# Converting double-precision weights by integer steps in a fused attention and SwiGLU kernel

## Chip, core and metric

The kernel runs on one core of a Trainium2 chip. The core has a matrix engine (TensorE, PE in the profile), a vector engine (VectorE, DVE), an activation engine (ScalarE, ACT), a general engine (GpSimd, POOL) and a queue that issues its transfers (SyncE, SP). The metric is the device time of one execution in microseconds (us). A difference under 0.5% can't be told from no change here.

## What is computed

The reference, cut to what matters:

```
a    = softmax(phi, over the 576 positions)            # phi (8, 8, 576, 32)
k_m, v_m = a^T k, a^T v                                # 32 memory rows per head
attn = softmax(q k_m^T / 8);  x = attn v_m             # 4608 rows x 512
xn   = x / sqrt(mean(x*x) + 1e-6) * rms_g
g, val = xn @ w_gate, xn @ w_val                       # w_*: (512, 1536)
out  = (g * sigmoid(g) * val) @ w_out                  # w_out: (1536, 512)
```

The inputs q, k, v, phi are float32, and the weights reach the core as 8-byte doubles: a low and a high 32-bit word for each number. The core has to make float32 of them itself.

## The kernel before

**Two stages.** The first stage, about 0 to 145 us, reads phi, k, v and q, builds the memory rows of all 8 batches and, for the first 4 batches, the attention weights. The second stage has 48 steps `i`: two passes over the 12 column blocks of the weights, each pass for two pairs of batches (`where(i)` gives pass, block pair `u`, batch pair `pr` and block `j`). A step multiplies a weight block by the value rows (`vw_steps`, 12 matmuls at L849), splits that product into a high and a low part (`xh` on ScalarE at L873, `xl` on VectorE at L874), multiplies it by the attention weights to get gate and value (`gv_steps`, 48 matmuls at L896), applies SiLU (`sg`, L904) and the product (`hf`, L905), splits again (`hh` L918, `hl` L919), and every second step multiplies by w_out (`out_steps`, 54 matmuls at L938, summed into `acc` at L943 on ScalarE or L945 on VectorE). The attention of the last 4 batches (L965 to L1035) is woven into the first pass.

**Conversion.** `convert(kind, n)` makes float32 of one 128x512 weight tile, kind 0 for w_gate, 1 for w_val, 2 for w_out; 12 blocks make 36 tiles. It happens in the first pass only; split tiles are stored to memory and loaded again in the second pass (`reload`). Before, a tile takes steps `s0` to `s4`. From the high word: the exponent bits by a mask (L345), clamped (L347), rescaled on ScalarE (L350), joined with the sign bit (L358). From both words: the fraction by a mask (L365), the low word added to it (L369), scaled to a number between 1 and 2 on ScalarE (L376). A product of the two (L385) is the weight `w`. That is six VectorE instructions, of which two tiles' last one runs on GpSimd (`PRM["CE"]`), and two on ScalarE. `s5` splits `w` into high (ScalarE, L402) and low (GpSimd, L403), `s6` stores them. `raw` tiles come from memory into two buffers; `ex` and `mi` have one buffer each, so that a tile's steps can start only when the tile before has let go of it.

**Order.** All pieces are placed on a time axis by the table `PRM` (offsets in `PRE`, `PSW`, `PI` for the conversions) and recorded in that order; the framework's scheduler then fixes the order on each engine. Each engine runs its list strictly in order.

**The first step.** For `i == 0` the value product has two one-bank PSUM tiles with the tag `o`; all other steps have one two-bank tile with the tag `vw`, of which there is one buffer. The banks of `vw` belong in the first stage to the tag `tr`, whose last user is the normalisation of the second batch pair (`rp`, read by VectorE at L212).

Of the kernel before, what the change touches and what calls it, by code (L numbers as in the profile page):

```python
# [1 line left out]

# [88 lines left out]
def kernel(  # L91
# [243 lines left out]
    def convert(kind, n):  # L335
# [4 lines left out]

        def s0():
            d["raw"] = t = raw.pop((kind, n))
            hw = t[:, :, 1]
# [1 line left out]
            V.tensor_scalar(out=ex, in0=hw, scalar1=0x7FF00000, scalar2=None, op0=ALU.bitwise_and)  # L345
            if (kind < 2 and n < 2 and PRM["CA"]) or ((kind == 2 or n >= 2) and PRM["CB"]):
                V.tensor_scalar(  # L347
                    out=ex, in0=ex, scalar1=float(896 << 20), scalar2=float(1151 << 20), op0=ALU.max, op1=ALU.min
                )
                nc.scalar.activation(ex, ex, AF.Copy, scale=8.0, bias=-float(896 << 23))  # L350
            else:
                V.tensor_scalar(out=ex, in0=ex, scalar1=float(-896 << 20), scalar2=0.0, op0=ALU.add, op1=ALU.max)

        def s1():
# [3 lines left out]
            V.scalar_tensor_tensor(  # L358
                out=ex, in0=d["raw"][:, :, 1], scalar=-(1 << 31), in1=ex,
                op0=ALU.bitwise_and, op1=ALU.bitwise_or,  # L360
            )

        def s2():
            d["m"] = m = wp[0].tile([P, 512], I32, tag="mi", name=f"mi{nm}")
            V.tensor_scalar(  # L365
                out=m, in0=d["raw"][:, :, 1], scalar1=0xFFFFF, scalar2=None, op0=ALU.bitwise_and
            )
# [1 line left out]
            V.scalar_tensor_tensor(  # L369
                out=mf, in0=d["raw"].bitcast(U32)[:, :, 0], scalar=2.0 ** -32, in1=m,  # L370
                op0=ALU.mult, op1=ALU.add,
            )
# [8 lines left out]

        def s4():
            m, ex = d["m"].bitcast(F32), d["ex"].bitcast(F32)
            on_pool = n < 2 and kind < 2 and PRM["CE"][n] & (1 << kind)
            (nc.gpsimd if on_pool else V).tensor_tensor(out=d["w"], in0=m, in1=ex, op=ALU.mult)  # L385
# [444 lines left out]
    def vw_steps(i):  # L830
# [2 lines left out]

        def mm(cc):
            def f():

# [8 lines left out]
                for e in range(2):
                    def lhs(vt):
                        return vt[:, cc, e].rearrange("p o x -> p (o x)")
                    for n, (l, r) in enumerate(((vh, wh), (vh, wl), (vl, wh))):
                        nc.tensor.matmul(  # L849
                            vp[:, e, :], lhs(l), r[:, 2 * cc + e, :],  # L850
                            start=(n == 0), stop=(n == 2),
                        )
            return f

        def evac():
            xh = sb.tile([P, 2, 2, 256], F32R, tag="xh", name=f"xh{i}", bufs=2)
            xl = sb.tile([P, 2, 2, 256], F32R, tag="xl", name=f"xl{i}", bufs=2)
            if i == 0:
                for cc, vp in enumerate(vw[i]):
                    halves = ((slice(0, 64), vp[:64]), (slice(64, P), vp[64:, ::-1, :]))  # L860
                    for rows, src in halves:
                        nc.scalar.copy(xh[rows, cc], src)
                    for rows, src in halves:
                        nc.vector.tensor_tensor(
                            out=xl[rows, cc], in0=src, in1=xh[rows, cc].bitcast(F32), op=ALU.subtract
                        )
                vw[i] = xh, xl
# [258 lines left out]
```

## Time and profile before

| what | value |
|---|---|
| time, median of 3 runs | 913.88 us (913.27 to 917.01) |
| span of the profiled execution, first to last instruction | 912.9 us |
| what lies around the span, by the median | about 1.0 us |
| TensorE busy | 837.6 us, 92% of the span |
| VectorE busy | 600.1 us, 66%, 1028 instructions |
| ScalarE busy | 421.2 us, 46% |
| GpSimd busy | 284.6 us, 31% |
| moved by transfers | 106.41 MB, mean 117 GB/s |

A row of a group gives the count, the busy time, the mean duration of one, and then the idle time of the engine just before these instructions with what ended it. A row of the table by windows gives, for each stretch, the busy time and count on each engine, the granted TensorE clock as a share of full speed, and the transfers. Matmuls overlap, so that a busy TensorE need not be one at its peak rate.

### The profile page before, as it was taken

The numbers are of one execution on the slowest core, as the hardware profiler recorded it, in microseconds if no ns is written. First come the engines' busy times: TensorE is split into PE (matmuls) and PEld (weight loads), VectorE is DVE, ScalarE is ACT, GpSimd is POOL, SyncE is SP. The second block draws the span as 40 slices with busy tenths as digits, with TensorE's granted clock in tenths as the row PEclk, the third lists the DMA queues.
The fourth block names the chain that finished last, engine by engine and source line by source line (L and its number), as shares of the span: only waits on it lengthen the run. The fifth ranks groups of instructions, "written<-read, shape, count | busy, mean of one in ns | idle before, by whom it ended". The sixth has DMA issues, their size and how long they took to land.

```text
span 912.9 us, 15844 instructions
## 1 busy us (share of the span) xinstructions
PE 837.6 (92%) x6207; PEld 740.8 (81%) x6207; DVE 600.1 (66%) x1028; ACT 421.2 (46%) x719; POOL 284.6 (31%) x242
## 2 busy tenths in 40 slices
PE   4989586899997999989999999999999999999997
PEld 4777475788886798878888897798889999999996
DVE  5578959998897876978765564732445454454543
ACT  2657334777755454666443352354424233243330
POOL 3464735432413233324232151312112121121120
PEclk9899788999999999999999999999999999999999
DMA  8976554354454341543314034311304013040046
GB/s 277 329 260 227 199 165 142 105 172 118 163 153 129 108 119 60 145 129 125 115 58 139 12 105 139 91 60 47 93 1 139 1 47 93 1 139 1 1 114 140
DMA packets 81506, 106.41 MB, mean 117 GB/s; under 512 B 34324, under 2 KB 52248, under 8 KB 81432
## 3 DMA queue, kind: packets, MB, share of 16 engines
q1 hardware_dynamic: 81432, 105.41, 37.6%
q8 instruction: 49, 0.80, 0.4%
q14 instruction: 25, 0.20, 0.1%
HBM read 73.93 MB, written 31.46 MB: 115 GB/s over the span
## 4 chain that ended last, share of the span: by engine, by line
PE 64%; DVE 20%; issue 5%; ACT 5%; DMA 4%; POOL 1%; SPq 0%; DVEq 0%; ACTq 0%; POOLq 0%
PE po L938 26%; PE pv L896 12%; PE pg L896 12%; PE vp L849 6%; PE kvp L573 3%; DVE xl L874 2%; DVE ex L345 2%; DVE mi L365 2%; DVE mi L369 2%; DVE ex L358 2%; DMA phi<-in_phi_dram 2%; DVE w L385 1%; PE xp L235 1%; DVE ex L347 1%; DVE acc L945 1%
## 5 line engine op out<-in xcount | busy, mean ns | idle before, releaser
L919 POOL TENSOR_TENSOR hl<-hf,hh 128x512 fp32r<-128x512 f32 (+1 forms) x96 | 139.8, 1457 | 422.3 <-ACT hh L918 409.3
L945 DVE TENSOR_TENSOR acc<-po,acc 128x512 f32<-128x512 f32 x180 | 123.0, 686 | 131.2 <-PE po L938 130.6
L938 PE MATMUL po<-oh,hh 128*128 128x512 f32 x432 | 174.0, 404 | 8.1 <-DVE acc L945 3.8
L938 PE MATMUL po<-ol,hh 128*128 128x512 f32 x432 | 170.8, 395 | 0.0
L938 PE MATMUL po<-oh,hl 128*128 128x512 f32 x432 | 170.7, 395 | 0.0
L904 ACT ACTIVATE sg<-pg 128x256 f32<-128x256 f32 x192 | 78.4, 409 | 161.7 <-PE pg L896 139.9
L874 DVE TENSOR_TENSOR xl<-vp,xh 64x1024 fp32r<-64x1024 f32 x94 | 114.7, 1220 | 47.9 <-ACT xh L873 46.4
L905 DVE TENSOR_TENSOR hf<-pv,sg 128x256 f32<-128x256 f32 x192 | 85.5, 453 | 72.4 <-PE pv L896 51.6
L873 ACT CAST xh<-vp 64x1024 fp32r<-64x1024 f32 x94 | 94.6, 1006 | 47.0 <-PE vp L849 22.4
L918 ACT CAST hh<-hf 128x512 fp32r<-128x512 f32 (+1 forms) x96 | 64.5, 673 | 85.2 <-DVE hf L905 59.4
L938 PEld LDWEIGHTS po<-oh,hh 128*128 128x128 f32 x432 | 81.3, 189 | 24.7 <-DVE acc L945 6.1
L938 PEld LDWEIGHTS po<-oh,hl 128*128 128x128 f32 x432 | 81.4, 189 | 19.6
L896 PE MATMUL pg<-ath,xh 128*128 128x320 f32 (+1 forms) x384 | 87.0, 300 | 9.3 <-ACT sg L904 4.9
L849 PE MATMUL vp<-wh,vm 128*128 128x256 f32 x384 | 85.6, 287 | 5.8 <-DVE xl L874 4.7
L938 PEld LDWEIGHTS po<-ol,hh 128*128 128x128 f32 x432 | 81.6, 189 | 11.0
L896 PE MATMUL pv<-ath,xh 128*128 128x320 f32 (+1 forms) x384 | 85.0, 300 | 2.6 <-DVE hf L905 2.4
L896 PE MATMUL pg<-ath,xl 128*128 128x320 f32 (+1 forms) x384 | 85.0, 296 | 0.1
L896 PE MATMUL pg<-atl,xh 128*128 128x320 f32 (+1 forms) x384 | 85.0, 296 | 0.0
L896 PE MATMUL pv<-atl,xh 128*128 128x320 f32 (+1 forms) x384 | 84.5, 296 | 0.0
L896 PE MATMUL pv<-ath,xl 128*128 128x320 f32 (+1 forms) x384 | 83.9, 296 | 0.0
L896 PEld LDWEIGHTS pg<-ath,xh 128*128 128x128 f32 x384 | 63.7, 189 | 16.4 <-ACT sg L904 7.1
L849 PEld LDWEIGHTS vp<-wh,vm 128*128 128x128 f32 x384 | 65.8, 190 | 9.7 <-DVE xl L874 2.7
(131 smaller groups left out, 1382.2 us busy)
## 6 DMA issues: line engine op xcount, KB each, us to landing
kv<-in_k_dram SPq DMA_DIRECT2D x32, 288.0 KB, 4.9
kv<-in_v_dram SPq DMA_DIRECT2D x32, 288.0 KB, 5.3
out_dram<-acc SPq DMA_DIRECT2D x72, 128.0 KB, 2.4
raw<-in_moe_w_gate_dram SPq DMA_DIRECT2D x12, 512.0 KB, 3.8
raw<-in_moe_w_val_dram SPq DMA_DIRECT2D x12, 512.0 KB, 3.7
wd<-wh SPq DMA_DIRECT2D x12, 512.0 KB, 3.0
wd<-wl SPq DMA_DIRECT2D x12, 512.0 KB, 3.3
raw<-in_moe_w_out_dram SPq DMA_DIRECT2D x12, 512.0 KB, 3.7
```

The lines of the kernel that those rows point to most:

```text
L345: V.tensor_scalar(out=ex, in0=hw, scalar1=0x7FF00000, scalar2=None, op0=ALU.bitwise_and)
L573: nc.tensor.matmul(kvp[64 * par:64 * par + 64, cc, 0:128], e_bd[j][:, hp, c, :], st["kv", b, hp][:, :, 64 * c:64 * c + 64], start=(c == 0) ...
L849: nc.tensor.matmul(vp[:, e, :], lhs(l), r[:, 2 * cc + e, :], start=(n == 0), stop=(n == 2),)
L873: nc.scalar.copy(xh[rows], src)
L874: nc.vector.tensor_tensor(out=xl[rows], in0=src, in1=xh[rows].bitcast(F32), op=ALU.subtract)
L896: nc.tensor.matmul(pt[:, :N], l[:, cc, b, half * P:half * P + P], r[:, b, cc, t0:t0 + n, :].rearrange("p t x -> p (t x)"), start=(m == 0), ...
L904: nc.scalar.activation(sg[:, :N], pg[:, :N], AF.Silu)
L905: nc.vector.tensor_tensor(out=hf[:, :, b, :], in0=pv[:, :N].rearrange("p (t x) -> p t x", x=64), in1=sg[:, :N].rearrange("p (t x) -> p t x ...
L918: nc.scalar.copy(hh, hv)
L919: nc.gpsimd.tensor_tensor(out=hl, in0=hv, in1=hh.bitcast(F32), op=ALU.subtract)
L938: nc.tensor.matmul(po, l[:, tt, :], r, start=(m == 0), stop=(m == 5))
L945: nc.vector.tensor_tensor(out=accs[key], in0=po, in1=accs[key], op=ALU.add)
```

## The change

`convert` is rewritten. The high word is read as a float32 on ScalarE (`Abs`), clamped on VectorE between two float constants whose bits are the old integer bounds, shifted left by 3 and masked, and joined with the two top bits of the raw word. The low word's top three bits, rounded, come from a ScalarE copy with a scale of 2^-29 into an integer tile. An integer addition of the two is the weight's bit pattern. That is four VectorE instructions a tile (or three and one on GpSimd) in place of six, and two on ScalarE as before; both ScalarE instructions now stand at the head of a tile and read `raw` from it. In the built program the addition on VectorE is an instruction on 16-bit halves, 1024 of them a partition. In the first step the value product is the two-bank tile that all others have.

```diff
+EXP_LO = struct.unpack("f", struct.pack("I", 896 << 20))[0]
+EXP_HI = struct.unpack("f", struct.pack("I", (1151 << 20) - 1))[0]
...
         def s0():
             d["raw"] = t = raw.pop((kind, n))
-            hw = t[:, :, 1]
             d["ex"] = ex = wp[0].tile([P, 512], I32, tag="ex", name=f"ex{nm}")
-            V.tensor_scalar(out=ex, in0=hw, scalar1=0x7FF00000, scalar2=None, op0=ALU.bitwise_and)
...
-                V.tensor_scalar(
-                    out=ex, in0=ex, scalar1=float(896 << 20), scalar2=float(1151 << 20), op0=ALU.max, op1=ALU.min
-                )
-                nc.scalar.activation(ex, ex, AF.Copy, scale=8.0, bias=-float(896 << 23))
...
+            nc.scalar.activation(ex.bitcast(F32), t.bitcast(F32)[:, :, 1], AF.Abs)
+            V.tensor_scalar(
+                out=ex.bitcast(F32), in0=ex.bitcast(F32), scalar1=EXP_LO, scalar2=EXP_HI,
+                op0=ALU.max, op1=ALU.min,
+            )
+            d["m"] = m = wp[0].tile([P, 512], I32, tag="mi", name=f"mi{nm}")
+            nc.scalar.activation(m, t.bitcast(U32)[:, :, 0], AF.Copy, scale=2.0 ** -29)

         def s1():
...
+            V.tensor_scalar(
+                out=ex, in0=ex, scalar1=3, scalar2=0x3FFFFFFF,
+                op0=ALU.logical_shift_left, op1=ALU.bitwise_and,
+            )
+        def s2():
             V.scalar_tensor_tensor(
-                out=ex, in0=d["raw"][:, :, 1], scalar=-(1 << 31), in1=ex,
+                out=ex, in0=d["raw"][:, :, 1], scalar=-(1 << 30), in1=ex,
                 op0=ALU.bitwise_and, op1=ALU.bitwise_or,
             )
-            V.tensor_scalar(
-                out=m, in0=d["raw"][:, :, 1], scalar1=0xFFFFF, scalar2=None, op0=ALU.bitwise_and
-            )
-            V.scalar_tensor_tensor(
-                out=mf, in0=d["raw"].bitcast(U32)[:, :, 0], scalar=2.0 ** -32, in1=m,
-                op0=ALU.mult, op1=ALU.add,
-            )

         def s3():
-            nc.scalar.activation(mf, mf, AF.Copy, scale=2.0 ** -20, bias=1.0)
...
         def s4():
-            (nc.gpsimd if on_pool else V).tensor_tensor(out=d["w"], in0=m, in1=ex, op=ALU.mult)
+            (nc.gpsimd if on_pool else V).tensor_tensor(out=d["w"].bitcast(I32), in0=d["m"], in1=d["ex"], op=ALU.add)
...
-                if i == 0:
-                    vw.setdefault(i, []).append(o_tile(f"vp{i}_{cc}").rearrange("p (e f) -> p e f", e=2))
-                elif cc == 0:
+                if cc == 0:
                     whole = ps.tile([P, 2, 2, 256], F32, tag="vw", name=f"vp{i}", bufs=1)
...
-            if i == 0:
-                for cc, vp in enumerate(vw[i]):
-                    ...  # four copies (L862), four subtractions (L864) of 64x512
-                return
```

The new instructions move the order. In the rows that follow, `ex2_0` is the tile `ex` of kind 2, block 0, and likewise `mi`, `w` and `raw_20`; `vp0` is the value product of step 0, `xh0` and `xl0` its parts.

VectorE where the first stage hands over to the second, before:

```order
L212 TENSOR_TENSOR at1_1503<-at1_1503,rp1_4_1770 128x1024
L385 TENSOR_TENSOR w1_1_1735<-mi1_1_1731,ex1_1_1726 128x512
L212 TENSOR_TENSOR at1_1503<-at1_1503,rp1_8_1776 128x256
L345 TENSOR_SCALAR ex2_0_1836<-raw_20_1724 128x512
L365 TENSOR_SCALAR mi2_0_1841<-raw_20_1724 128x512
L347 TENSOR_SCALAR ex2_0_1836<-ex2_0_1836 128x512
L369 SCALAR_TENSOR_TENSOR mi2_0_1841<-raw_20_1724,mi2_0_1841 128x512
L864 TENSOR_TENSOR xl0_1827<-vp0_0_1812,xh0_1826 64x512 x2
L358 SCALAR_TENSOR_TENSOR ex2_0_1836<-raw_20_1724,ex2_0_1836 128x512
L864 TENSOR_TENSOR xl0_1827<-vp0_1_1819,xh0_1826 64x512 x2
L385 TENSOR_TENSOR w2_0_1847<-mi2_0_1841,ex2_0_1836 128x512
```

and after:

```order
L217 TENSOR_TENSOR at1_1502<-at1_1502,rp1_4_1762 128x1024
L379 ISA w1_1_1727<-mi1_1_1723,ex1_1_1720 128x1024
L217 TENSOR_TENSOR at1_1502<-at1_1502,rp1_8_1768 128x256
L350 TENSOR_SCALAR ex2_0_1823<-ex2_0_1823 128x512
L359 TENSOR_SCALAR ex2_0_1823<-ex2_0_1823 128x512
L366 SCALAR_TENSOR_TENSOR ex2_0_1823<-raw_20_1718,ex2_0_1823 128x512
L379 ISA w2_0_1832<-mi2_0_1826,ex2_0_1823 128x1024
L854 TENSOR_TENSOR xl0_1818<-vp0_1804,xh0_1817 64x1024
L350 TENSOR_SCALAR ex2_1_1962<-ex2_1_1962 128x512
L359 TENSOR_SCALAR ex2_1_1962<-ex2_1_1962 128x512
L366 SCALAR_TENSOR_TENSOR ex2_1_1962<-raw_21_1733,ex2_1_1962 128x512
L854 TENSOR_TENSOR xl0_1818<-vp0_1804,xh0_1817 64x1024
```

The whole of tile 2_0 now stands ahead of the first `xl0`, and three steps of tile 2_1 between the two halves of `xl0`.

ScalarE at the same place, before:

```order
L402 CAST wh1_1720<-w1_1_1735 128x4x128
L223 CAST ath1_1783<-at1_1503 128x2x64 x2
L862 CAST xh0_1826<-vp0_0_1812 64x512 x2
L350 ACTIVATE ex2_0_1836<-ex2_0_1836 128x512
L862 CAST xh0_1826<-vp0_1_1819 64x512 x2
L376 ACTIVATE mi2_0_1841<-mi2_0_1841 128x512
L402 CAST oh0_2035<-w2_0_1847 128x512
L873 CAST xh1_1901<-vp1_1849 64x1024
L904 ACT_TABLE_LOAD
L904 ACTIVATE sg0_00_1871<-pg0_00_1857 128x256
```

and after:

```order
L396 CAST wh1_1714<-w1_1_1727 128x4x128
L349 ACTIVATE ex2_0_1823<-raw_20_1718 128x512
L355 ACTIVATE mi2_0_1826<-raw_20_1718 128x512
L228 CAST ath1_1775<-at1_1502 128x2x64 x2
L853 CAST xh0_1817<-vp0_1804 64x1024
L349 ACTIVATE ex2_1_1962<-raw_21_1733 128x512
L355 ACTIVATE mi2_1_1965<-raw_21_1733 128x512
L396 CAST oh0_2018<-w2_0_1832 128x512
L853 CAST xh0_1817<-vp0_1804 64x1024
L349 ACTIVATE ex0_2_2048<-raw_02_1830 128x512
L355 ACTIVATE mi0_2_2051<-raw_02_1830 128x512
L884 ACT_TABLE_LOAD
```

Between the two halves of `xh0` stand two conversion steps of tile 2_1 and the copy `oh0` of tile 2_0's weight, and the head of tile 0_2 stands ahead of the first SiLU.

VectorE in the middle of the first pass, block 7 of w_gate, before:

```order
L385 TENSOR_TENSOR w1_6_3673<-mi1_6_3667,ex1_6_3656 128x512
L345 TENSOR_SCALAR ex0_7_3750<-raw_07_3598 128x512
L365 TENSOR_SCALAR mi0_7_3756<-raw_07_3598 128x512
L347 TENSOR_SCALAR ex0_7_3750<-ex0_7_3750 128x512
L874 TENSOR_TENSOR xl10_3473<-vp10_3399,xh10_3472 64x1024
L369 SCALAR_TENSOR_TENSOR mi0_7_3756<-raw_07_3598,mi0_7_3756 128x512
L945 TENSOR_TENSOR acc0_5_2329<-po5_5_3106,acc0_5_2329 128x512
L358 SCALAR_TENSOR_TENSOR ex0_7_3750<-raw_07_3598,ex0_7_3750 128x512
L1012 TENSOR_REDUCE mx2_3_0_3168<-S2_3_0_3157 128x10
L874 TENSOR_TENSOR xl10_3473<-vp10_3399,xh10_3472 64x1024
L385 TENSOR_TENSOR w0_7_3762<-mi0_7_3756,ex0_7_3750 128x512
```

and after:

```order
L379 ISA w1_6_3628<-mi1_6_3616,ex1_6_3613 128x1024
L992 TENSOR_REDUCE mx2_3_5_3168<-S2_3_5_3134 128x8
L854 TENSOR_TENSOR xl10_3435<-vp10_3360,xh10_3434 64x1024
L993 TENSOR_TENSOR ex2_3_3119<-S2_3_5_3134,mx2_3_5_3168 128x256
L350 TENSOR_SCALAR ex0_7_3705<-ex0_7_3705 128x512
L925 TENSOR_TENSOR acc0_6_2399<-po5_6_3171,acc0_6_2399 128x512
L359 TENSOR_SCALAR ex0_7_3705<-ex0_7_3705 128x512
L1005 TENSOR_REDUCE sm2_3_3225<-ex2_3_3119 128x18
L366 SCALAR_TENSOR_TENSOR ex0_7_3705<-raw_07_3556,ex0_7_3705 128x512
L1006 TENSOR_SCALAR sm2_3_3225<-sm2_3_3225 128x18
L925 TENSOR_TENSOR acc0_7_2414<-po5_7_3185,acc0_7_2414 128x512
L379 ISA w0_7_3715<-mi0_7_3708,ex0_7_3705 128x1024
```

The four steps of a tile keep their place among the work that TensorE waits for (`acc`, `xl`); the two masks at its head and the fraction's sum are gone.

More of the change, by code (lines that the diff above doesn't have):

```diff
@@ L1 @@
+import struct
 from contextlib import ExitStack, nullcontext
@@ L354, in s1 @@
+            V.tensor_scalar(
[4 more added lines that the diff above has]
+            nc.scalar.activation(m, t.bitcast(U32)[:, :, 0], AF.Copy, scale=2.0 ** -29)
         def s1():
             ex = d["ex"]
-            if not ((kind < 2 and n < 2 and PRM["CA"]) or ((kind == 2 or n >= 2) and PRM["CB"])):
-                V.tensor_scalar(out=ex, in0=ex, scalar1=float(255 << 20), scalar2=8.0, op0=ALU.min, op1=ALU.mult)
+            V.tensor_scalar(
+                out=ex, in0=ex, scalar1=3, scalar2=0x3FFFFFFF,
+                op0=ALU.logical_shift_left, op1=ALU.bitwise_and,
+            )
@@ L358, in s1 @@
+        def s2():
+            ex = d["ex"]
             V.scalar_tensor_tensor(
-                out=ex, in0=d["raw"][:, :, 1], scalar=-(1 << 31), in1=ex,
+                out=ex, in0=d["raw"][:, :, 1], scalar=-(1 << 30), in1=ex,
                 op0=ALU.bitwise_and, op1=ALU.bitwise_or,
             )
-        def s2():
-            d["m"] = m = wp[0].tile([P, 512], I32, tag="mi", name=f"mi{nm}")
-            V.tensor_scalar(
-                out=m, in0=d["raw"][:, :, 1], scalar1=0xFFFFF, scalar2=None, op0=ALU.bitwise_and
-            )
-            mf = m.bitcast(F32)
-            V.scalar_tensor_tensor(
-                out=mf, in0=d["raw"].bitcast(U32)[:, :, 0], scalar=2.0 ** -32, in1=m,
-                op0=ALU.mult, op1=ALU.add,
-            )
@@ L374, in s3 @@
         def s3():
-            mf = d["m"].bitcast(F32)
-            nc.scalar.activation(mf, mf, AF.Copy, scale=2.0 ** -20, bias=1.0)
             if kind < 2 and n < 2:
@@ L382, in s4 @@
         def s4():
-            m, ex = d["m"].bitcast(F32), d["ex"].bitcast(F32)
             on_pool = n < 2 and kind < 2 and PRM["CE"][n] & (1 << kind)
-            (nc.gpsimd if on_pool else V).tensor_tensor(out=d["w"], in0=m, in1=ex, op=ALU.mult)
+            (nc.gpsimd if on_pool else V).tensor_tensor(out=d["w"].bitcast(I32), in0=d["m"], in1=d["ex"], op=ALU.add)
         def s5():
@@ L857, in evac @@
             xl = sb.tile([P, 2, 2, 256], F32R, tag="xl", name=f"xl{i}", bufs=2)
-            if i == 0:
-                for cc, vp in enumerate(vw[i]):
[L860 to L867, printed above, removed]
-                return
             vp = vw[i][2]
```

3 lines of the change are left out of this document (removed).

## The prediction

> **What bounds the kernel now.** I read the page's slices first, to see who is full when, then the table by windows. After the busy times (PE, PEld, DVE, ACT, POOL) a row of that table ends with the granted TensorE clock, the transfers' share and their GB/s.
>
> ```profile
> PE 837.6 (92%) x6207; PEld 740.8 (81%) x6207; DVE 600.1 (66%) x1028; ACT 421.2 (46%) x719; POOL 284.6 (31%) x242
> ...
> DVE  5578959998897876978765564732445454454543
> ```
> ```profile
> 160.00:460.00 300.00, 278.88 (x1920) 245.91 (x1920) 255.36 (x404) 183.15 (x308) 99.37 (x72) 0.99 0.41 125
> 460.00:640.00 180.00, 175.64 (x1150) 154.67 (x1149) 91.92 (x184) 72.97 (x133) 52.96 (x47) 1.00 0.28 83
> 640.00:900.00 260.00, 258.96 (x1584) 235.17 (x1584) 129.84 (x191) 88.00 (x146) 53.10 (x37) 1.00 0.20 60
> 76.00:120.00 44.00, 31.16 (x443) 26.33 (x441) 40.74 (x85) 22.25 (x42) 26.56 (x30) 0.84 0.50 172
> ```
>
> Slices 8 to 20, 160 to 460 us, hold the conversions: VectorE is busy 255.4 of 300 us (85%) there, 51% in 460 to 640, and 50% in 640 to 900, where TensorE leaves 1 us free. TensorE's own 279 us in the conversion window says little, since overlapping matmuls are counted busy while they wait in their pipeline. So I count what its matmuls need, from the stretch where nothing holds them: the end of the chain of waits, and the rows of L938 alone.
>
> ```profile
> 893.77 14.02 PE po L938 x60
> ```
> ```profile
> 160.00:460.00 300.00, 115.21 (x432) 77.31 (x432) 0.99 0.41 125
> 460.00:640.00 180.00, 81.30 (x312) 55.75 (x312) 1.00 0.28 83
> 640.00:900.00 260.00, 134.08 (x520) 93.42 (x521) 1.00 0.20 60
> ```
> ```profile
> 158.12 0.60 PE L984 MATMUL qtp<-ident,qr 128*128 128x128 f32 x4
> 186.26 0.80 PE L1002 MATMUL S<-km,qT 128*64 128x64 f32 x20
> ```
>
> One L938 matmul is 14.02 / 60 = 0.234 us. In 640 to 900 the other 1584 - 520 = 1064 have (260 - 520 x 0.234) / 1064 = 0.130 us each. In 160 to 460 there are 432 of L938 (101 us) and 1488 others; those at L1002 number 288 at 0.80 / 20 = 0.04 us (12 us), those at L984 72 at 0.15 us (11 us), and 1128 are at 0.130 (147 us). That is 270 of 300 us: TensorE loses about 30 us in the conversion window. The same count for 460 to 640 (312, 642 at 0.130, 196 attention matmuls at a mean of about 0.07) gives 170 of 180, so 10 us or 5.5% are lost with VectorE only half full. That much seems to be the price of the weaving itself: 16.5 us in 300.
>
> Who ends TensorE's idle time, and whose work stands on the chain, both in 160 to 460:
>
> ```profile
> PE pg L896 <- ACT sg L904: 4.9, 5, 1.9
> PE vp L849 <- DVE xl L874: 4.4, 4, 1.6
> PE po L938 <- DVE acc L945: 3.8, 4, 1.5
> PE pv L896 <- DVE hf L905: 1.9, 2, 1.7
> ```
> ```profile
> by line: PE po L938 12.6%; issue 11.8%; PE pv L896 7.1%; PE pg L896 6.3%; DVE xl L874 5.8%; DVE ex L345 5.7%; DVE mi L365 4.7%; DVE mi L369 4.6%; DVE ex L358 4.3%; PE vp L849 3.9%; DVE ex L347 3.6%; DVE hf L905 3.5%; DVE w L385 3.5%; DVE ac
> ```
>
> TensorE waits for `xl`, `acc` and `hf`, which stand in VectorE's list behind conversion steps, and those steps are themselves a quarter of the chain.
>
> **The six instructions that become four.** VectorE's groups in 160 to 460 (count, busy us, mean ns, idle before), and two lines over the whole run (minimum/median/maximum ns):
>
> ```profile
> L874 DVE TENSOR_TENSOR xl<-vp,xh 64x1024 fp32r<-64x1024 f32 x39 | 47.6, 1219 | 8.8 <-ACT xh L873 8.1
> ...
> L385 DVE TENSOR_TENSOR w<-mi,ex 128x512 f32<-128x512 f32 x30 | 28.4, 948 | 2.5 <-POOL ol L403 0.8 <-POOL wl L403 0.5
> L358 DVE SCALAR_TENSOR_TENSOR ex<-raw,ex 128x512 int32<-128x512 int32 x31 | 26.3, 848 | 1.7 <-ACT ex L350 1.2
> L369 DVE SCALAR_TENSOR_TENSOR mi<-raw,mi 128x512 f32<-128x512 uint32 x30 | 24.3, 810 | 0.0
> L345 DVE TENSOR_SCALAR ex<-raw 128x512 int32<-128x512 int32 x30 | 22.5, 750 | 0.4
> L365 DVE TENSOR_SCALAR mi<-raw 128x512 int32<-128x512 int32 x30 | 19.4, 646 | 0.0
> L347 DVE TENSOR_SCALAR ex<-ex 128x512 int32<-128x512 int32 x30 | 17.6, 588 | 0.0
> ```
> ```profile
> L345 DVE TENSOR_SCALAR ex<-raw x36: 408/428/1681, 81.8 to 440.6; 128x512 int32<-128x512 int32 x36
> ```
> ```profile
> L385 DVE TENSOR_TENSOR w<-mi,ex x34: 670/693/2041, 89.1 to 463.9; 128x512 f32<-128x512 f32 x34
> ```
>
> Gone are L345, L365 and L369: 22.5 + 19.4 + 24.3 = 66.2 us in the window. The clamp stays (L347's price), the join stays (L358's), the addition takes the place of the product L385, and one shift-and-mask is new. It has one source and one result of 128x512 in the core's memory, like L347 and L365: 17.6 to 19.4 us for 30. So VectorE loses about 47 us, 1.6 us a tile: 255 becomes 208, or 69%.
>
> The same shape takes 428 ns in the median and up to 1681 where it meets GpSimd's work. [...]
>
> The addition is not shown in this trace: 1024 16-bit elements a partition from two sources. If two are done at once it is like L385 with 512; if one at a time, like L874 with 1024: 0.69 to 1.22 us, which is 0 to 0.53 x 30 = 16 us more. I take 0, since its bytes are exactly L385's, and keep the other as a rival. [...]
>
> What of the 47 us reaches the end? At most the chain's own share: 5.7 + 4.7 + 4.6% less a shift's 3.6% is 11.4% of 300, or 34 us. By the count above, TensorE loses 30 us at 85% and at VectorE's half load 16.5. At 69%, a straight line between the two would give 7.9% of 300 = 24, a gain of 6 us; but waiting in a queue falls fastest near full load, and the shed work stands directly on the chain, which speaks for the upper half of 6 to 34. I take **16 us**: the whole excess of 13.5 over the half-loaded stretch, and a few of the 16.5, since the part of the conversion after 460 and the stored pieces come earlier too.
>
> **ScalarE's two instructions.**
>
> ```profile
> L350 ACT ACTIVATE ex<-ex 128x512 int32<-128x512 int32 x31 | 19.6, 631 | 38.0 <-DVE ex L347 38.0
> L873 ACT CAST xh<-vp 64x1024 fp32r<-64x1024 f32 x38 | 38.2, 1004 | 17.1 <-PE pv L896 8.6 <-PE vp L849 5.5 <-DVE xl L874 2.5
> ```
>
> Two of 128x512 stay two; those now read every second word. If that costs nothing they take 0.63 us, if it doubles the path 1.00 as L873 does: 0 to 0.37 x 60 = 22 us on an engine at 183 of 300. I cost it at nothing; ScalarE's 117 idle us cover it, and without them `sg` and `xh` would be late. They move to the tile's head. A tile's `Abs` waits for `raw` and for the release of the one `ex`, by the addition of the tile before. `xh` and `sg` stand behind it. Before, L350 made them wait in the same way, 38.0 us in all; that wait was for L347 and goes.
>
> **The first stage.** Three tiles convert before L532, in a stretch where VectorE is busy 40.7 of 44 us.
>
> ```profile
> 113.53 1.38 DVE L365 TENSOR_SCALAR mi<-raw 128x512 int32<-128x512 int32 x1
> ...
> 117.46 1.34 DVE L532 TENSOR_TENSOR phi<-phi,mr 128x1152 f32<-128x1152 f32 x1
> ...
> 128.75 0.43 DVE L345 TENSOR_SCALAR ex<-raw 128x512 int32<-128x512 int32 x1 [4.54 <-DMA raw<-in_moe_w_val_dram]
> 129.09 0.42 DVE L365 TENSOR_SCALAR mi<-raw 128x512 int32<-128x512 int32 x1
> 129.76 0.42 DVE L347 TENSOR_SCALAR ex<-ex 128x512 int32<-128x512 int32 x1
> 130.10 0.69 DVE L369 SCALAR_TENSOR_TENSOR mi<-raw,mi 128x512 f32<-128x512 uint32 x1
> ```
> ```profile
> 129.96 1.34 PE L235 MATMUL xp<-gb,at 128*64 128x128 f32 x10 [4.03 <-DVE ssq L248]
> ```
>
> Undisturbed, a tile sheds 0.43 + 0.42 + 0.69 - 0.42 = 1.12 us; with one step as dear as the 1.38, 2.1. Three tiles give 3.4 to 6. If the landing that TensorE waits 4.03 us for stays where it is, 0. I take **3 us**: the load is issued after this stretch and moves with it.
>
> **The first step's tile and the hand-over.** The two-bank tile takes banks of `rp`, so that `vp0` can't start before the last L212 ends.
>
> ```profile
> 143.87 0.39 PE L849 MATMUL vp<-wh,vm 128*128 128x256 f32 x1
> ...
> 152.07 0.58 PE L896 MATMUL pg<-ath,xh 128*128 128x256 f32 x1 [3.22 <-ACT xh L862]
> ```
> ```profile
> 145.86 0.41 DVE L212 TENSOR_TENSOR at<-at,rp 128x256 f32<-128x256 f32 x1
> ```
> ```profile
> 160.17 0.38 ACT L904 ACTIVATE sg<-pg 128x256 f32<-128x256 f32 x1
> ```
>
> L212 ends at 146.27, so `vp0` starts 2.4 us later; the second gate product, at 152.07, also waits behind two ScalarE steps of tile 2_1 that need the addition of 2_0. That is 3 us there, but the first `sg` at 160.17 follows a wait for other work, and the pieces of TensorE that run early in between are not lost. Bounds 0 (all within the 3.22 us) and +3; I take **+1.5**, the middle.
>
> **The sum.** The profiled span of 912.9 and about 1.0 around it are the median of the runs shown, 913.9. Less 3, plus 1.5, less 16: **896 us**.
>
> **The rivals.**
> *All of VectorE's stalls go.* The chain's 34 us come out whole: 913.9 - 1.5 - 34 = 878, range 870 to 884. For it, the waits named above end on VectorE; against it, the 5.5% lost at half load.
> *The addition runs one element at a time.* 16 us come back on VectorE, 75% full; two fifths to two thirds of the 16 stay: 902 to 908.
> *No change.* The stalls hang on ScalarE, the transfers and the fixed order, as from 460 to 640: only a few us go, 910 to 917. For it, `sg` ends the largest wait of the list above, 4.9.
> *Slower: ScalarE's queue.* `Abs` stands in front of `xh` and `sg` and waits for the tile before or for its transfer, where nothing else may pass. The gain of 17.5 us over 30 tiles breaks even at 0.58 us a tile that reaches TensorE; at 1 us a tile 896 becomes 926. Against it, the 38 us that L350 waited at the same place already.
>
> **How the numbers follow.** 0.5%, or 4.6 us, is about what can be told from no change. The forecast (884 to 909) has a chance of 0.60, all stalls gone 0.10, the slow addition 0.08, no change 0.10, ScalarE's queue 0.12. The first three are faster: 0.78; same 0.10; slower 0.12. The range 878 to 914 leaves out half of the first rival and the last one, and the edges of the forecast's own.
>
> **What the changed profile would show.** Right: VectorE busy near 545 us (600.1 in the first row above, less 47 and six tiles' 8 outside the window), additions of about 0.69 us in the median, ScalarE's two steps near 0.63, the count of TensorE's lost time from 30 to about 14 us in 300, and the second gate product of step 0 some 1.5 to 3 us late against the work before it. Wrong: additions of 1.2 us; `Abs` waiting for the addition or a transfer with `pg` waiting for `sg` behind it for more than 10 us in sum; or a TensorE that idles as before with VectorE at 70%.

## Result and the profile after

The changed kernel takes 902.42 us (median of 4 runs, 899.68 to 903.85) against 915.27 us before (median of 4, 913.27 to 917.01): ratio 0.986, 95% interval 0.9835 to 0.9885. It is faster by 12.9 us where 17.9 were forecast.

The page of the changed kernel; the lines answer to those of before:

```profile
span 899.7 us, 15784 instructions
...
PE 837.1 (93%) x6207; PEld 742.7 (83%) x6207; DVE 559.7 (62%) x954; ACT 422.5 (47%) x717; POOL 285.4 (32%) x242
...
DVE  5577948884787877778845746522445455454543
```

The table by windows, and the rows of the output matmuls alone (now L918):

```profile
160.00:460.00 300.00, 289.36 (x2030) 258.46 (x2030) 229.76 (x356) 190.22 (x318) 107.46 (x79) 1.00 0.41 128
460.00:640.00 180.00, 175.75 (x1130) 154.92 (x1129) 87.41 (x173) 72.18 (x128) 48.72 (x41) 0.99 0.30 87
```
```profile
160.00:460.00 300.00, 118.51 (x450) 80.04 (x450) 1.00 0.41 128
```

In the 300 us of the conversion TensorE now gets through 2030 matmuls instead of 1920. Counted as in the prediction (450 at 0.234 us, 1196 at L840 and L876 at 0.130, 288 at 0.04, 96 at 0.15) they need 287 us: 13 us lost where 30 were. From 460 to 640 nothing is won: 314 at 0.234, 642 at 0.130 and 174 at 0.07 need 169 of 180 us, 11 lost against 10.

VectorE's groups in 160 to 460, then the addition over the whole run:

```profile
L379 DVE CUSTOM_DVE_ANT_0 w<-mi,ex 128x1024 uint16<-128x1024 uint16 x30 | 33.1, 1103 | 4.3 <-POOL wl L397 2.5 <-DVE ex L366 1.2 <-POOL ol L397 0.4
L366 DVE SCALAR_TENSOR_TENSOR ex<-raw,ex 128x512 int32<-128x512 int32 x29 | 23.1, 795 | 0.3
L350 DVE TENSOR_SCALAR ex<-ex 128x512 f32<-128x512 f32 x29 | 23.0, 793 | 4.7 <-ACT ex L349 4.2
L359 DVE TENSOR_SCALAR ex<-ex 128x512 int32<-128x512 int32 x29 | 15.6, 538 | 0.5
```
```profile
L379 DVE CUSTOM_DVE_ANT_0 w<-mi,ex x34: 672/694/2014, 88.7 to 449.5; 128x1024 uint16<-128x1024 uint16 x34
```

The four groups sum to 94.8 us where the six of before summed to 138.5. The 1024 halves of the addition take 694 ns in the median, as the 512 products did (693); its mean in the window is 1103 where the product's was 948.

Who ends TensorE's idle time, and whose work is on the chain, in the same window:

```profile
PE po L918 <- DVE acc L925: 4.1, 5, 1.4
PE pg L876 <- ACT sg L884: 2.2, 2, 1.5
PE vp L840 <- DVE xl L854: 1.7, 3, 1.0
```
```profile
by line: PE po L918 25.7%; PE pv L876 16.0%; PE pg L876 15.1%; PE vp L840 7.7%; issue 6.6%; DVE xl L854 3.4%; DVE ex L350 3.0%; DVE w L379 2.7%; PE S L982 1.8%; ACT xh L853 1.7%; DVE acc L925 1.6%; DVE hf L885 1.5%; DVE ex L366 1.5%; PE qtp
```

The waits for `sg` and `xl` fell to less than half (4.9 and 4.4 us before) and that for `hf` from 1.9 to 0.2; the one for `acc` did not fall (3.8 before). The conversion on VectorE was a quarter of the chain and is 7% with the three groups that the row shows (3.0 + 2.7 + 1.5; the fourth stands lower than the row reaches); the matmuls of L918, L876 and L840 are 65% of it, up from 30%.

The first stage and the hand-over, TensorE's waits:

```profile
101.21 1.09 PE L209 MATMUL rp<-ident,rinv 128*128 128x128 f32 x4 [4.35 <-DVE rinv L281]
...
129.66 3.56 PE L240 MATMUL xp<-gb,at 128*64 128x128 f32 x32 [3.25 <-ACT gram L645]
140.53 1.09 PE L209 MATMUL rp<-ident,rinv 128*128 128x128 f32 x8 [1.97 <-DVE rinv L281]
145.59 0.39 PE L840 MATMUL vp<-wh,vm 128*128 128x256 f32 x1 [2.35 <-DVE at L217]
154.65 0.80 PE L876 MATMUL pg<-ath,xh 128*128 128x256 f32 x2 [6.86 <-ACT xh L853]
```

The same places before, as far as not yet shown:

```profile
104.09 1.94 PE L204 MATMUL rp<-ident,rinv 128*128 128x128 f32 x8 [5.64 <-DVE rinv L276]
...
141.23 1.09 PE L204 MATMUL rp<-ident,rinv 128*128 128x128 f32 x8 [1.97 <-DVE rinv L276]
```

The changed kernel is 2.9 us ahead at the first `rp`, 0.3 at `xp` and 0.7 at the second `rp`; it is 1.7 behind at `vp0` and 2.6 behind where the second half of `xh0` is waited for (before, the second gate product, at 152.07). Before, two gate and two value products had already run from 148.11 on with the first half; each half is now 64 rows of the whole product, so that no gate product can start before both are there.

### The profile page after: what moved, and what is told of

Read it like the earlier page. It is cut to its first block, busy times and chain, and to the rows that moved or that the text cites. A ratio compares the mean times of both kernels' runs of the same rounds, so it can differ in the third digit from the quotient of the medians.

```text
span 899.7 us, 15784 instructions
## 1 busy us (share of the span) xinstructions
PE 837.1 (93%) x6207; PEld 742.7 (83%) x6207; DVE 559.7 (62%) x954; ACT 422.5 (47%) x717; POOL 285.4 (32%) x242
## 4 chain that ended last, share of the span: by engine, by line
PE 76%; DVE 11%; DMA 4%; ACT 4%; issue 3%; SPq 0%; POOL 0%; ACTq 0%; DVEq 0%; POOLq 0%
PE po L918 30%; PE pv L876 15%; PE pg L876 15%; PE vp L840 7%; PE kvp L567 3%; PE xp L240 2%; DMA phi<-in_phi_dram 2%; DVE xl L854 1%; DVE ex L350 1%; DVE w L379 1%; DVE acc L925 1%; DMA raw<-in_moe_w_val_dram 1%; DVE ex L366 1%; PE qtp L679 1%; PE S L700 1%
## 5 line engine op out<-in xcount | busy, mean ns | idle before, releaser
L918 PE MATMUL po<-oh,hh 128*128 128x512 f32 x432 | 173.3, 402 | 5.9 <-DVE acc L925 4.1
L918 PE MATMUL po<-oh,hl 128*128 128x512 f32 x432 | 170.9, 396 | 0.0
L918 PE MATMUL po<-ol,hh 128*128 128x512 f32 x432 | 170.8, 395 | 0.0
L854 DVE TENSOR_TENSOR xl<-vp,xh 64x1024 fp32r<-64x1024 f32 x96 | 117.0, 1219 | 55.1 <-ACT xh L853 54.0
L853 ACT CAST xh<-vp 64x1024 fp32r<-64x1024 f32 x96 | 96.7, 1008 | 57.4 <-DVE xl L854 29.3
L918 PEld LDWEIGHTS po<-oh,hh 128*128 128x128 f32 x432 | 81.4, 189 | 21.3 <-DVE acc L925 6.9
L918 PEld LDWEIGHTS po<-oh,hl 128*128 128x128 f32 x432 | 81.4, 189 | 19.5
L876 PE MATMUL pg<-ath,xh 128*128 128x320 f32 (+1 forms) x384 | 87.0, 300 | 9.1 <-ACT xh L853 6.9
L918 PEld LDWEIGHTS po<-ol,hh 128*128 128x128 f32 x432 | 81.5, 189 | 11.1
L840 PE MATMUL vp<-wh,vm 128*128 128x256 f32 x384 | 85.7, 286 | 4.2 <-DVE at L217 2.3
L876 PE MATMUL pg<-ath,xl 128*128 128x320 f32 (+1 forms) x384 | 85.7, 296 | 0.0
L876 PE MATMUL pg<-atl,xh 128*128 128x320 f32 (+1 forms) x384 | 85.7, 297 | 0.0
L876 PE MATMUL pv<-ath,xh 128*128 128x320 f32 (+1 forms) x384 | 84.3, 299 | 0.7 <-DVE hf L885 0.6
L876 PE MATMUL pv<-atl,xh 128*128 128x320 f32 (+1 forms) x384 | 84.6, 296 | 0.0
L876 PE MATMUL pv<-ath,xl 128*128 128x320 f32 (+1 forms) x384 | 82.6, 296 | 0.0
L876 PEld LDWEIGHTS pg<-ath,xh 128*128 128x128 f32 x384 | 63.5, 190 | 13.9 <-ACT xh L853 7.2
L840 PEld LDWEIGHTS vp<-wh,vm 128*128 128x128 f32 x384 | 66.2, 191 | 7.5 <-DVE xl L854 3.0
```

Source lines behind the costliest of these rows:

```text
L840: nc.tensor.matmul(vp[:, e, :], lhs(l), r[:, 2 * cc + e, :], start=(n == 0), stop=(n == 2),)
L853: nc.scalar.copy(xh[rows], src)
L854: nc.vector.tensor_tensor(out=xl[rows], in0=src, in1=xh[rows].bitcast(F32), op=ALU.subtract)
L876: nc.tensor.matmul(pt[:, :N], l[:, cc, b, half * P:half * P + P], r[:, b, cc, t0:t0 + n, :].rearrange("p t x -> p (t x)"), start=(m == 0), ...
L918: nc.tensor.matmul(po, l[:, tt, :], r, start=(m == 0), stop=(m == 5))
```

## Experiments

The second `rp` (141.23 and 140.53 above) is the last place ahead of the hand-over. Its start divides each profiled execution in two: what comes before is the first stage, and span less that start is "the rest" below. Each ratio is to the kernel before.

| kernel | ratio, 95% interval | VectorE busy | second rp at | rest |
|---|---|---|---|---|
| before | 1 | 600.1 | 141.2 | 771.7 |
| changed | 0.986 (0.9835 to 0.9885) | 559.7 | 140.5 | 759.2 |
| e1 old first tile | 0.9822 (0.9798 to 0.9845) | 559.2 | 138.2 | 757.7 |
| e2 first tile alone | 0.994 (0.9926 to 0.9954) | 590.9 | 144.6 | 765.0 |
| e3 three instructions back | 1.0173 (1.0139 to 1.0207) | 621.3 | 141.8 | 786.7 |
| e4 two instructions out | 0.9731 (0.9708 to 0.9753) | 506.0 | 136.2 | 751.0 |
| e5 two buffers | 0.995 (0.993 to 0.997) | 555.4 | 142.0 | 767.5 |
| e6 early w_val | 0.9925 (0.9899 to 0.9951) | 561.4 | 142.9 | 761.5 |
| e7 old tile, two buffers | 0.9899 (0.9875 to 0.9923) | 556.8 | 142.2 | 762.5 |
| e8 PI | 0.9998 (0.9982 to 1.0013) | 598.8 | 141.6 | 771.1 |
| e9 warm hand-over | 0.9864 (0.9844 to 0.9885) | 555.9 | 140.3 | 758.7 |
| e10 old tile, warm | 0.9842 (0.9819 to 0.9865) | 559.2 | 143.3 | 757.1 |
| e11 before, SU | 0.9965 (0.994 to 0.999) | 596.4 | 141.1 | 768.1 |
| e12 changed, SU | 0.9888 (0.9866 to 0.9909) | 559.1 | 142.1 | 761.5 |

Two readings of the table come first. The kernels changed, e1, e5, e7, e9, e10 and e12 issue the same instructions in the same order on every engine up to the second `rp`, yet it starts at 138.2 to 143.3 us: the first stage scatters by 5 us from one execution to another. The rest scatters far less, as far as two pairs can tell: 771.7 and 771.1 for before and e8, whose orders are the same; 757.7 and 757.1 for e1 and e10, which differ by 16 matmuls. So what concerns the second stage is read from the rest.

**e1: the conversion alone.**

```diff
-                if cc == 0:
+                if i == 0:
+                    vw.setdefault(i, []).append(o_tile(f"vp{i}_{cc}").rearrange("p (e f) -> p e f", e=2))
+                elif cc == 0:
...
+            if i == 0:
+                for cc, vp in enumerate(vw[i]):
+                    ...  # the four copies and four subtractions of the first step
+                return
```

> The changed kernel with the first step's value product in two one-bank tiles again; the integer conversion stays. In the changed kernel the first value matmul starts at 145.59 us (143.87 before) and the second gate product at 154.65 (152.07 before). Theory A (the conversion's lighter VectorE load brings the gain, the two-bank tile costs about 2.5 us at the hand-over): first value matmul near 143.2, ratio to before about 0.983, 899 to 901 us. Rival (the first-step tile is part of the gain, or indifferent): ratio 0.986 or above, 902 us or more.

Measured 0.9822 (897.61 us), a little under theory A's time. The rest is 14.0 us shorter than before's (757.7 against 771.7), so that the conversion alone carries the gain, together with the order that comes with it. Against the changed kernel it is 1.5 us shorter in the rest; the other 2.4 us by which its profiled execution ends earlier lie in the first stage, whose list is the same. The 4.8 us between the medians (902.42 and 897.61) are therefore not all the tile's, and the two intervals overlap.

**e2: the first-step tile alone.** The edit is the reverse of e1's, on the kernel before.

> The kernel before with only the first step's two-bank tile. Theory A: the first value matmul moves to about 146.3, 2.4 us later, and the kernel is 1 to 3 us slower than before (ratio 1.001 to 1.003). Rival (the tile or the new order that it sets off brings part of the gain): ratio 0.997 or lower.

Measured 0.994: faster, against theory A's sign. The tile's price at the hand-over is there (`vp0` starts 4.5 us after the second `rp`, 2.6 before), but TensorE has a different order from then on (532 lines), and the rest is 6.7 us shorter. e8, e11 and e12 take up what such an order is worth.

**e3: three instructions more on VectorE.**

```diff
                 op0=ALU.logical_shift_left, op1=ALU.bitwise_and,
             )
+            for _ in range(2):
+                V.tensor_scalar(out=ex, in0=ex, scalar1=0x3FFFFFFF, scalar2=None, op0=ALU.bitwise_and)
...
+            V.scalar_tensor_tensor(
+                out=ex, in0=d["raw"][:, :, 1], scalar=-(1 << 30), in1=ex,
+                op0=ALU.bitwise_and, op1=ALU.bitwise_or,
+            )
```

> The changed kernel with three VectorE instructions a tile added back, of the shapes that were removed (two one-source 128x512 masks, one two-source 128x512 mask-and-or; each repeats what is already in the tile, so that the values stay). ScalarE, the first-step tile and the head of the tile stay as changed. Theory A (VectorE's load is the cause): the gain goes, ratio 0.998 to 1.004, VectorE about 620 us busy, about 14 us more lost by TensorE in 160 to 460 us. Rival (the gain is from ScalarE's new place, a shorter dependency chain or the order): ratio stays 0.985 to 0.990.

Measured 1.0173, 930.28 us. ScalarE's new place, which stays, does not keep the gain. The size was forecast too low, since four and three are seven instructions a tile and not the six of before. The table by windows, and TensorE's largest waits there:

```profile
160.00:460.00 300.00, 276.32 (x1874) 244.81 (x1874) 264.16 (x417) 179.66 (x299) 102.84 (x71) 0.97 0.40 122
```
```profile
PE po L924 <- DVE acc L931: 6.3, 4, 3.6
PE pg L882 <- ACT sg L890: 4.0, 3, 2.0
PE pv L882 <- DVE hf L891: 3.1, 4, 1.3
```

Two things come along with the three instructions. A tile's chain is longer as well, and holds the one `ex` longer: `Abs` waits 37.4 us for the addition here and 18.9 in the changed kernel. And the granted clock is 0.97 in this window where the changed kernel has 1.00, which makes up to 9 us of the 300. So the run shows what added conversion work costs, but not how much of it is VectorE's time alone.

**e4: two instructions fewer.** The shift with its mask and the join are left out, so that the weights have no proper exponent and sign.

```diff
-            V.tensor_scalar(
-                out=ex, in0=ex, scalar1=3, scalar2=0x3FFFFFFF, ...)
-            V.scalar_tensor_tensor(
-                out=ex, in0=d["raw"][:, :, 1], scalar=-(1 << 30), in1=ex, ...)
```

> The changed kernel without the shift-and-mask and the join of every tile (two more VectorE instructions a tile left out, so that the weights have no proper exponent and sign); all else stays. Their price in the changed kernel's window of 160 to 460 us is 15.6 + 23.1 us. Adding 62 us to VectorE (559 to 621) cost 28 us, or 0.45 us for each. Theory A (VectorE's queue, with a gain that shrinks as the queue empties): VectorE about 510 us busy, ratio to before 0.974 to 0.980, 892 to 897 us. Rival (a straight line at 0.45): 880 us, ratio 0.961. Rival (what is left hangs on ScalarE, GpSimd and the order): ratio 0.984 to 0.988.

Measured 0.9731, 890.63 us, a little under theory A's range. In the rest, 61.6 us more VectorE work (e3) cost 27.5 us, 0.45 for each, the lower clock included; 53.7 us less (e4) brought 8.2 us, 0.15 for each. The count of TensorE's lost time in 160 to 460 us, with the prediction's prices, says the same: 3 us in e4, 13 in the changed kernel, 30 before and 38 in e3, with VectorE busy 189, 230, 255 and 264 us. What the conversion costs falls off as VectorE empties, which is what the prediction rested on.

**e5 and e7: two buffers for ex and mi**, e5 on the changed kernel, e7 on e1.

```diff
+            late = kind == 2 or n >= 2
+            odd = late and (n % 2 if kind == 2 else kind)
-            d["ex"] = ex = wp[0].tile([P, 512], I32, tag="ex", name=f"ex{nm}")
+            d["ex"] = ex = (sb if odd else wp[0]).tile([P, 512], I32, tag="cx" if odd else "ex", name=f"ex{nm}")
...  # mi in the same way
```

> The changed kernel with two buffers each for ex and mi in the second stage, used in turn, so that Abs of a tile needn't wait for the addition of the tile before (18.9 us in 13 waits in the window of 160 to 460 us, up to 3.8 us). Theory C (ScalarE's queue holds xh and sg behind Abs and costs time): Abs's wait falls under 5 us, ratio 0.978 to 0.982. Theory A (those waits are covered): Abs's wait falls just so, ratio stays 0.983 to 0.989.

> The kernel with the old first tile and the integer conversion (897.6 us), with two buffers each for ex and mi in the second stage. Theory C: 893 to 896 us. Theory A: 896 to 900 us, that is the two-buffer edit changes nothing beyond what a new order does.

Both theories missed: 0.995 and 0.9899, slower by 8.6 us than the kernel each started from (911.05 and 902.42; 906.23 and 897.61). In the rest the two differ, 8.3 and 4.8 us. ScalarE's wait, in the changed kernel and in e5:

```profile
ACT ex L349 <- DVE w L379: 18.9, 13, 3.8
```
```profile
ACT ex L351 <- DVE w L381: 8.3, 7, 3.7
```

It went down by 10.6 us, though not under the 5 us that were expected, and brought nothing. VectorE's timeline in e5 shows one thing that came instead:

```profile
297.69 0.62 DVE L927 TENSOR_TENSOR acc<-po,acc 128x512 f32<-128x512 f32 x1
298.23 1.11 DVE L361 TENSOR_SCALAR ex<-ex 128x512 int32<-128x512 int32 x1
299.27 2.03 DVE L381 CUSTOM_DVE_ANT_0 w<-mi,ex 128x1024 uint16<-128x1024 uint16 x1
301.22 0.68 DVE L368 SCALAR_TENSOR_TENSOR ex<-raw,ex 128x512 int32<-128x512 int32 x1
301.82 0.68 DVE L927 TENSOR_TENSOR acc<-po,acc 128x512 f32<-128x512 f32 x1
```

Steps of two tiles (the shift and the join of one, between them the addition of another) stand in a row of 3.6 us between two `acc`, which can't come about with one buffer each. TensorE waits for that `acc`, and then runs at half its clock (TensorE alone, stretches of 1 us; the columns are busy time, granted clock, transfers):

```profile
302.56 0.50 PE L920 MATMUL po<-oh,hh 128*128 128x512 f32 x1 [2.53 <-DVE acc L927]
```
```profile
300.00:301.00 1.00, 0.03 (x1) 1.00 0.64 147
...
303.00:304.00 1.00, 1.00 (x5) 0.59 0.74 187
304.00:305.00 1.00, 1.00 (x4) 0.50 0.94 328
305.00:306.00 1.00, 1.00 (x3) 0.50 0.03 9
306.00:307.00 1.00, 1.00 (x4) 0.71 0.00 0
307.00:308.00 1.00, 1.00 (x10) 1.00 0.00 0
```

After 2.5 us of waiting, the lower clock takes 0.41 + 0.50 + 0.50 + 0.29 = 1.7 us of work more. The whole window in e5, whose third number from the end is the clock:

```profile
160.00:460.00 300.00, 283.42 (x1984) 254.87 (x1983) 221.66 (x352) 188.03 (x313) 102.11 (x74) 0.98 0.42 128
```

The clock was 1.00 there in the changed kernel. The 2% of 300 us come to at most 6 of the 8.6 us; TensorE's listed waits in the window add up to 16 us where the changed kernel has 10. That the second buffers cause this through the order is read from the trace; no run keeps the order and changes the buffers alone, and e7's 4.8 us are hardly more than what an order alone is worth below.

**e6: the second w_val tile loaded earlier.**

```diff
-            + convert(0, 0) + [lambda: load_w(0, 1)] + convert(1, 0) + [lambda: load_w(1, 1)]
+            + convert(0, 0) + [lambda: load_w(0, 1)] + convert(1, 0)
...
+        ev.append((PRM["CV"] + PRM["CP"] * (len(w) - 4) , lambda: load_w(1, 1)))
         w = second_weights()
```

> The changed kernel with one load moved: the second w_val tile is issued ahead of four k and v loads in SyncE's queue instead of behind them. In the changed kernel it landed at 127.97 us, where ScalarE's Abs had waited 2.88 us for it, gram stood behind Abs, and TensorE waited 3.25 us for gram, so that the 2.9 us won at 101 us were 0.3 us at 129.7. Theory B (that landing swallowed the first stage's gain): the wait goes, the first value matmul comes 2 to 3 us earlier, ratio about 0.983, 899 to 901 us. Rival (the k and v loads are then late instead, or rinv and at hold the hand-over anyway): ratio 0.985 to 0.988.

Measured 0.9925, slower than the changed kernel. ScalarE in the changed kernel, then in e6:

```profile
127.97 0.66 ACT L349 ACTIVATE ex<-raw 128x512 f32<-128x512 f32 x1 [2.88 <-DMA raw<-in_moe_w_val_dram]
...
129.34 0.27 ACT L645 COPY gram<-kvt 128x128 f32<-128x128 f32 x1
```
```profile
124.58 0.66 ACT L349 ACTIVATE ex<-raw 128x512 f32<-128x512 f32 x1 [6.28 <-DMA raw<-in_moe_w_val_dram]
125.14 0.57 ACT L199 COPY at<-tp 128x512 f32<-128x512 f32 x1
```
```profile
125.77 1.98 PE L240 MATMUL xp<-gb,at 128*64 128x128 f32 x16 [5.75 <-ACT at L199]
```

The tile landed 3.4 us earlier, but the scheduler moved `Abs` even further forward, ahead of the copies of `at`, and ScalarE waited 6.28 us with those behind it; TensorE waited 5.75 us for `at`. Neither theory was tested as meant. It does show that `Abs`, waiting for a load at the head of ScalarE's list, holds up TensorE by way of what is queued behind it.

**e8, e11 and e12: what an order is worth.** One number of the table each: e8 `PI=0.0257` on the kernel before, e11 and e12 `SU[0]=1.774` on the kernel before and on the changed one.

> The kernel before with one number of the table changed (PI 0.0157 to 0.0257, the spacing of a tile's steps on the time axis); no instruction is added or removed, a few hundred rows change places on VectorE, ScalarE and TensorE. It tells what an order alone is worth. The first-step tile alone made the kernel before faster by 0.6%, which nothing in its own price explains. If orders differ by several us: ratio off 1 by 0.003 to 0.01 on either side, with the difference in TensorE's lost time between 160 and 460 us. If the order is worth nothing: 0.998 to 1.002, and the two-bank tile itself must have brought the 0.6%.

> The kernel before with the first attention piece of the last batches placed 0.1 step earlier on the time axis (SU[0] 1.874 to 1.774). No instruction is added or removed; the order of 452 lines changes on TensorE, 184 on VectorE, 149 on ScalarE, about as much as the first-step tile alone changes (532, 236, 177), and the hand-over stays. Theory E (an order alone is worth several us, and the 0.6% of the first-step tile alone was such an order): ratio off 1 by 0.003 to 0.01 on either side. Rival (the two-bank tile itself helps the old conversion): 0.998 to 1.002.

> The changed kernel with the same number changed (SU[0] 1.874 to 1.774); 301 lines change on TensorE, 54 on VectorE, 76 on ScalarE. It says how far the changed kernel's 0.986 hangs on its order. Theory E: 0.980 to 0.992. Rival (with VectorE a third empty the order no longer matters): 0.985 to 0.987.

e8 turned out to be a repeat: by operation and tile name, the lists of all engines are the same in its trace as before. Its 0.9998 says how well equal kernels agree. e11 did reorder (452 lines on TensorE) and gave 0.9965, 3.6 us shorter in the rest; e12 gave 0.9888, 2.3 us longer than the changed kernel, with overlapping intervals. So in these two cases an order was worth 2 to 4 us, one way and the other, in the rest, with no instruction added or removed. e2's 6.7 us are larger than that; whether the tile helps the old conversion beyond its order is open.

**e9 and e10: keeping TensorE busy at the hand-over**, 40 extra matmuls on the changed kernel, 16 on e1.

```diff
+                    if i == 0 and gi == 0 and b == 0:
+                        wu = wsplit[0][0].rearrange("p hp g f -> p hp (g f)")
+                        for _ in range(40):
+                            nc.tensor.matmul(pg[:, :256], vm[pr][:, 0][:, 0, 0].rearrange("p o x -> p (o x)"),
+                                             wu[:, 0, :], start=True, stop=True)
                     for half, pt in ((0, pg), (1, pv)):
```

> The changed kernel with 40 extra matmuls of 128x256 into step 0's gate tile, ahead of its real ones (which overwrite them), in the time in which TensorE waits for xh0. In the changed kernel TensorE stood still for 6.86 us there and its granted clock was 0.50 from 147 to 160 us, so that 5.4 us of work after the wait ran at half speed; before, the clock was 0.50 from 150 to 156. Theory D (the hand-over's price is doubled by the clock): clock at 1.00 by 154 us, 2 to 3 us less, ratio 0.982 to 0.984, 899 to 900 us. Rival (VectorE and ScalarE set the pace there, the clock costs nothing): ratio 0.985 to 0.988.

> The integer conversion with the old first tile (897.6 us) and 16 extra matmuls of 128x256 into step 0's gate tile, overwritten by the real ones; TensorE's order is otherwise the same. TensorE waited 2.19 us there, with a mean granted clock of 0.89 in 140 to 160 us. Theory D: clock 0.97 to 1.00 in that stretch, 1 to 2 us less, ratio 0.980 to 0.981. Rival (the clock costs nothing): ratio 0.982 to 0.984.

TensorE alone, in the changed kernel and in e9, and e9's wait for the second half of `xh0`:

```profile
147.00:154.00 7.00, 0.80 (x4) 0.50 0.72 201
154.00:161.00 7.00, 6.35 (x32) 0.56 1.09 328
```
```profile
147.00:154.00 7.00, 4.25 (x36) 0.97 0.59 179
154.00:161.00 7.00, 5.70 (x28) 0.54 1.09 342
```
```profile
155.30 0.80 PE L881 MATMUL pg<-ath,xh 128*128 128x256 f32 x2 [4.04 <-ACT xh L853]
```

The extra matmuls held the clock at 0.97 while they ran and were over 4.04 us too early: it was down to 0.54 again when the real work came. In e10 it was 0.91 and 0.84 in the same two stretches, against 0.76 and 1.00 in e1. e9's ratio equals the changed kernel's, and e10's rest equals e1's within 0.6 us. So the test of theory D failed to set its own condition, and what the clock costs at the hand-over stays open.

## Why the prediction came out as it did

**The first pass (forecast 16 us).** By the rest, e1 and e10 (757.7, 757.1) against before and e8 (771.7, 771.1) give 14.0 us. The way it goes is shown from both sides: more conversion work costs 0.45 us for each us of VectorE, less brings 0.15. The 14.0 us are those of a new order too, which alone was worth 2 to 4 us in e11 and e12, so the size is known no better than that. The count said 30 us lost would become 14, and it became 13, but not by the prediction's reasoning: VectorE is at 77% and not at 69% in the window, and the 16.5 us taken as the price of the weaving itself, from 5.5% lost at half load, are no floor, since the changed kernel loses 4.4% and e4, with VectorE at 63%, 1%. The two errors go against each other, and that the number came out is partly luck. Why 460 to 640 us loses more with VectorE half empty is open. The "all stalls go" rival, 34 us, is out for this change: with two more instructions removed (e4) the whole gain against before was still only 20.7 us in the rest.

**VectorE's load was mis-sized.** Forecast: busy near 545 us in the whole run, 208 in the window; measured 559.7 and 229.8. The prediction subtracted groups from the busy time, but in the window of before the groups of VectorE add up to 278.8 us and the engine was busy 255.4: neighbours overlap by some 8%, so that a removed group frees less than its own sum. Over the whole run the conversion's instructions on VectorE add up to 166.1 us before and 114.5 after, 51.6 less, and the busy time falls by 40.4. The conversion groups shed 43.7 us (138.5 to 94.8) and not 47: the clamp, taken at L347's price, has a mean of 793 ns where L347 had 588, and the addition 1103 where the product had 948; the join and the shift came out cheaper. That the new instructions would be held up as the old ones were, which pricing by means takes for granted, was an estimate. It held: of the 36 at L345 before, the 16 during which GpSimd ran nothing took 408 to 439 ns and the other 20 took 415 to 1681, and of the 34 additions on VectorE the 16 without GpSimd at work took 672 to 694 and the other 18 took 672 to 2014. And the window now holds 6% more matmuls, with their `xl`, `acc` and `hf`.

**The addition (rival at 8%).** It ran as forecast, 694 ns in the median against 693 for 512 products: the fast value, 0.69 us, and not the slow one, 1.22. How many elements it does at once the trace does not show. Its spread, 672 to 2014 ns, is the product's (670 to 2041).

**The first stage (forecast 3 us) is the step that failed.** Shedding 2.9 us by the first `rp` was right. "The load is issued after this stretch and moves with it" was half right: it was issued 2.8 us earlier (119.73 against 122.57) and landed 0.8 us earlier (127.97 against 128.75):

```profile
122.57 0.38 SPq L298 DMA_DIRECT2D raw<-in_moe_w_val_dram  x1
```
```profile
119.73 0.38 SPq L303 DMA_DIRECT2D raw<-in_moe_w_val_dram  x1
```

In e1, issued at 119.46, `Abs` began at 125.63. The landing takes 6 to 8 us with an identical list. Over the seven executions with the integer conversion and this first stage the first `rp` stands at a mean of 102.5 us and the second at 141.2; over the four with the old one (before, e2, e8, e11) at 104.9 and 142.1. So 2.4 us are won and 0.9 remain, with a scatter of 5: not to be told from nothing. In all eleven the second `rp` stands 12.0 to 13.8 us after the first use of this tile, so that the end of the first stage goes with the landing; in the mean the load is issued 1.8 us earlier and its first use comes 1.1 us earlier.

**The hand-over (forecast +1.5).** The rest of changed and e9 (759.2, 758.7) against e1 and e10 gives 1.6 us. The gate product that waits for the second half of `xh0` came 2.6 us late on the span's time axis, but the forecast of 1.5 to 3 us was "against the work before it": counted from the second `rp` it starts after 14.1 us where it started after 10.8, 3.3 us late. The agreement of the 1.6 us with the forecast is partly luck, since the order after it differs too, and orders are worth 2 to 4 us.

**The sum.** -14.0, +1.6 and -0.9 make -13.3 us; measured are 12.9 between the medians and 13.2 between the spans. Two of the missing 5 us are the first stage, two the first pass. The median of the kernel before, 913.88 when the prediction was made, came to 915.27 with one run more, which moved the predicted number by another 1.4 us to the low side.

**The rival of ScalarE's queue (12%).** `Abs` waits as feared, 18.9 us in 13 waits, but `pg` waits less for `sg` than before (2.2 against 4.9 us), and taking the wait away (e5, e7) made the kernel slower. The condition named, 10 us of `pg` waiting for `sg`, is not met.

## What to carry to other kernels

Work shed from an engine that others queue behind pays by how full that engine is: here 0.45 us for each us between 560 and 621 us of VectorE time, and 0.15 between 506 and 560. What the bound engine loses in the stretch itself bounds the gain better than the work removed does, but a half-empty stretch with other work in it is no measure of the loss that will remain. A wait on a single buffer may be what keeps the steps of two tiles apart; look at what will stand in the queue in its place before it is removed. Where a scheduler writes the order, compare stages from a common point, repeat an equal kernel, and hold effects of a few us to be the order's until shown otherwise.
